# Saved tensors in another DRAM layout without row copies, and a forward softmax in two halves of heads, in a recurrent-memory transformer's forward and backward pass

## The chip, the cores and the metric

The kernel runs on one core of a Trainium2 chip. The core has a matrix engine (TensorE; in the profile PE for its matmuls, PEld for its weight loads), VectorE (DVE), ScalarE (ACT), GpSimd (POOL) and SyncE (SP), which here issues most of the DMAs (its queue is SPq in the rows). Sixteen DMA engines carry the transfers of the core. The metric is the device time of one execution in microseconds. Before: 2802.92 us, the median of three runs (2802.28 to 2803.98).

## The reference

The kernel computes a layer's output and all ten gradients (x, mem0, Wq, Wk, Wv, Wo, w1, b1, w2, b2) for a given grad_out. Cut to what matters:

```python
def _A_ref(x, mem0, Wq, Wk, Wv, Wo, seg_len):      # S 2048, Dm 512, 32 heads of 128, M 8, seg 32
    mask = (idx[:, None] < M) | (idx[:, None] >= idx[None, :])
    mem = mem0
    for s in range(S // seg_len):                  # 64 segments, one after the other
        h = concatenate([mem, x[:, s*32:(s+1)*32]], axis=1)      # 40 rows
        q, k, v = (einsum('btd,dhe->bhte', h, W) for W in (Wq, Wk, Wv))
        p = softmax(where(mask, q @ k^T * scale, -1e9))
        o = einsum('bhte,hed->btd', p @ v, Wo)
        mem = o[:, :M]                             # the memory of the next segment
        outs.append(o[:, M:])

def _B_ref(x, w1, b1, w2, b2):                     # F 1792
    return square(relu(x @ w1 + b1)) @ w2 + b2

xn = layernorm(x)
out = x + _A_ref(xn, ...) + _B_ref(xn, ...)        # and the gradients of all that by jax.vjp
```

## The kernel before

The work is done in five stages. First layer norm and the MLP, forward and the part of backward that needs no attention. Then the forward scan: 64 steps, one for each segment, each of which needs the memory that the step before gave. Four steps make a block (SPB = 4; 16 blocks, TC = 16). Then the attention weights are turned for backward. Then the backward scan over the 64 steps in the other direction. Last, the gradients of the four attention weights as large matmuls, which read what the scans saved in DRAM.

In a step 32 rows (RA; 8 of memory and the last 24 tokens) of 32 heads are worked on as 128 partitions by 1024 columns: the heads form four quarters (JQ = 4), quarter j on partitions 32 j to 32 j + 31, and 8 heads of 128 columns (NI = 8) lie side by side in a quarter. The first 8 tokens of each of a block's four segments ("L" rows, names that end in L) are computed once for a block, beside the chain of steps.

A forward step (`chain`, L1136) projects q, k and v (`proj`), copies them out of PSUM (`evict`, L526, one VectorE or ScalarE copy for 512 columns), transposes q and k on TensorE (`to_T`, L546), multiplies them into one PSUM bank of scores (`ps_sc`) on top of the mask, does softmax (`weights` L1003, `sums` L1012, `normalize` L1017), transposes the weights on VectorE, forms O = P V (`diag`, which scales by one over the sum), transposes O (`sq_T`), multiplies by Wo (`wo_part`) and turns the new memory into the next step's input (`ps_mem`). Into the gaps the stage puts matmuls of the MLP's weight gradients (`dw_unit`), whose inputs come as tiles `anT` and `sx`.

Each step saves to DRAM, by SyncE's queue: S_V, S_K, S_Q, S_P, S_ON (its O). Two DRAM-to-DRAM copies a step gather the memory rows of K and V (S_KM, S_VM) for the block's L rows. More row copies gather rows for the last stage (S_HNA, S_HNL, S_GOA, S_GOL) and the output's L rows (S_OL, S_BL).

A backward step loads those tensors (`load`: bP, VR by a transposing DMA, bqN, bkN), computes the gradients of q, k and v (dN, three of them, stored as S_GN), the parts of the L rows (eL, stored in S_GNL, read back as dLN) and the gradient of the layer's input.

The order of the three scheduled stages does not come from the code's order. Operations are recorded with their reads and writes and a cost for each engine that could do them; a planner (`_Plan`) lays them out in time with these costs, a rank along the longest path, a table of corrections for each operation (BIAS) and three numbers (PAR), and then emits them in the order it found. Each engine's queue is executed in that order. All DMAs that the steps name go through one helper (L477):

```python
def dma(self, out_f, in_f, R, W, prio=1, lat=3.2, cost=T_DMA, eng="SP"):
    q = {"SP": nc.sync, "POOL": nc.gpsimd, "ACT": nc.scalar}[eng]
    self.plan.add({eng: cost}, lambda e: q.dma_start(out_f(), in_f()), R, W, prio, lat)
```

so almost every DMA has line L479 in the profile, and copies out of PSUM have L433 (VectorE) or L435 (ScalarE).

Of the kernel before, what the change touches and what calls it, by code (L numbers as in the profile page):

```python
# [10 lines left out]
PAR = ((0.3, 0.3, 0.0), (0.61, 7.94, 4.04), (0.09, 2.05, 17.32))  # L11
BIAS_0 = None
BIAS_1 = {
    "l_proj": (
        47.2, 6.5, -41.1, 1.2, 0.8, -33.9, -14.2, 11.4, 20.3, -5.1, -5.3, -14.4, 17.4, 1.5, 7, 20.1, 4.7,
        25.3, -22.2, 55.6, -37, 19.3, -97.5, -1.4, 23, -6.1, -29.3, 48.8, 4.1, 4.5, 52.1, -159.3,
    ),
    "blk_in": (
        11.4, -35.6,
    ),  # L20
# [4 lines left out]
    ),  # L25
    "chain": (
# [4 lines left out]
    ),  # L31
    "blk_out": (
        16.8, -102.8, -36.2, -171.6, -10.2, -72.7, -50.6, -74.7, -96.5, 48.6,
    ),
    "l_attn": (
# [16 lines left out]
    ),  # L52
    "l_pre": (
        46.2, 1.1, -8.1, -100.3, 71, -115.1, -66.8, -4.6, 0.3, -83.5, 0.5, -9.3, -80.7, -12.7, -35.4, -15.9,
        26.3, 9.2, -131.2, 6, 10.9, -47, -9.6, -40.9, 6.9, -128.5, -6.9, -9.4, -61.5, 28.5, -31.2, -38.8,
        -146.2,
    ),
    "load": (
# [33 lines left out]

class _PE(dict):
    shape = None
    n = 8


def pe(cost, shape, n=8):
# [10 lines left out]
class _Plan:  # L109
# [56 lines left out]
    def run(self):  # L166
# [52 lines left out]
        while elig:  # L219
# [48 lines left out]
            if o.shape:  # L268
                shape = o.shape
# [1473 lines left out]
```

## Time and profile before

| what | value |
| --- | --- |
| time, median of three runs | 2802.92 us |
| the profiled execution: span from first to last instruction | 2798.3 us |
| TensorE busy | 2664.6 us (95%), clock 0.995 |
| VectorE / ScalarE / GpSimd busy | 1327.3 / 985.8 / 824.8 us |
| bytes moved by DMA | 530.91 MB, mean 190 GB/s |
| forward scan | about 228 to 1202 us |
| backward scan | about 1235 to 2225 us |
| weight gradients | about 2238 us to the end |

A row of the profile names line, engine, operation, tile written and tiles read, then a count and times. A window row (one for each stretch A:B) lists its length, then busy time and count of instructions of PE, PEld, DVE, ACT and POOL, the granted TensorE clock, the mean busy share of the sixteen DMA engines and GB/s. The bytes of a packet are put down where the packet starts. Issues of DMAs by SyncE are told in a timeline as start and duration of the issue, not of the transfer.

### The profile page before, as it was taken

What the parts mean: (1) busy time and instruction counts of PE and PEld (TensorE: products, weight loads), DVE (VectorE), ACT (ScalarE), POOL (GpSimd) and SP (SyncE); (2) the same over time, 40 slices, a digit from 0 to 9 for tenths busy, and PEclk for the clock granted to TensorE, in tenths of its full rate; (3) what the DMA queues carried; (4) which work ended last, traced back from release to release, by engine and by line L of the source; (5) the groups of instructions that cost most, each with busy time, mean ns of one, the idle gap of its engine ahead of it and who ended that gap; (6) DMA issues with size and microseconds to landing.
All of it is one profiled execution on the core that took longest, in us unless ns stands there. A gap on an engine that the chain in (4) does not pass through costs nothing.

```text
span 2798.3 us, 125071 instructions
## 1 busy us (share of the span) xinstructions
PE 2664.6 (95%) x54888; PEld 1538.5 (55%) x55072; DVE 1327.3 (47%) x3327; ACT 985.8 (35%) x2012; POOL 824.8 (29%) x2431
## 2 busy tenths in 40 slices
PE   8998999999999999999999999999999899999999
PEld 6664555555555555575555555555555444444444
DVE  5544455555455555565455455555455402232322
ACT  4333444444444444364444444444444300000000
POOL 1111111111111111145555555555555301112210
PEclk9999999999999999999999999999999999999999
DMA  6657656555557566647777676777766698788861
GB/s 211 202 172 205 180 160 175 164 166 163 156 169 186 169 185 175 177 118 178 187 181 187 179 189 179 189 192 190 188 182 177 201 344 273 232 255 270 257 185 42
DMA packets 499792, 530.91 MB, mean 190 GB/s; under 512 B 223845, under 2 KB 325398, under 8 KB 497070
## 3 DMA queue, kind: packets, MB, share of 16 engines
q1 hardware_dynamic: 480254, 463.06, 59.9%
q0 software_dynamic: 15056, 53.56, 5.6%
q8 instruction: 430, 7.05, 1.1%
q10 hardware_dynamic: 3936, 6.29, 0.7%
q14 instruction: 116, 0.95, 0.1%
HBM read 249.77 MB, written 237.52 MB: 174 GB/s over the span
## 4 chain that ended last, share of the span: by engine, by line
PE 45%; DVE 4%; issue 3%; DMA 3%; ACT 1%; POOL 1%; SPq 0%; DVEq 0%; ACTq 0%; POOLq 0%
PE ps_gw L1690 14%; PE ps_dRA L1370 8%; PE ps_gw L1694 5%; PE ps_gO L538 3%; PE ps_dRL L1370 3%; PE ps_d L624 2%; DMA dLN<-S_GNL 2%; PE ps_d L573 1%; PE ps_d L599 1%; PE ps_gOT L429 1%; PE ps_d L588 1%; PE ps_gm L1524 1%; PE ps_gL L538 1%; PE ps_dL L1481 1%; PE ps_dP L1468 1%
## 5 line engine op out<-in xcount | busy, mean ns | idle before, releaser
L1370 PE MATMUL ps_dRA<-WA,dT 128*32 128x512 bf16 x6144 | 377.0, 381 | 5.3 <-issue 2.5
L1690 PE MATMUL ps_gw<-WA,WB 128*128 128x512 bf16 x1505 | 330.6, 379 | 1.6
L1690 PEld LDWEIGHTS <-WB 128*128 128x128 bf16 x1896 | 185.4, 98 | 225.0 <-issue 1.7
L538 PEld LDWEIGHTS <-PA 128*32 128x32 bf16 x8192 | 195.4, 96 | 192.3 <-DVE PA L1190 22.3
L435 ACT CAST dN<-ps_d 128x512 bf16<-128x512 f32 x372 | 207.4, 590 | 184.7 <-PE ps_d L599 112.3
L1370 PEld LDWEIGHTS <-dT 128*32 128x32 bf16 x6144 | 151.8, 96 | 154.2 <-DVE dT L517 17.3
L433 DVE CAST gwo<-ps_gw 128x512 bf16<-128x512 f32 x64 | 40.0, 685 | 399.9 <-PE ps_gw L1690 268.5
L435 ACT CAST gwo<-ps_gw 128x512 bf16<-128x512 f32 x64 | 33.1, 598 | 510.2 <-PE ps_gw L1690 357.3
L517 DVE STREAM_TRANSPOSE dT<-dN 128x256 f32<-128x256 f32 x384 | 165.4, 437 | 72.1 <-ACT dN L435 66.5
L1020 POOL TENSOR_TENSOR P<-P,rsA 128x320 bf16<-128x320 bf16 x64 | 46.2, 722 | 458.8 <-DVE rsA L1015 244.1
L624 PEld LDWEIGHTS <-PB 32*32 32x32 bf16 x8192 | 119.8, 92 | 76.4 <-DVE PB L1168 23.9
L1701 POOL DMA_DIRECT2D out_dram<-gwo x96 | 71.6, 753 | 293.9 <-ACT gwo L435 265.1
L538 PE MATMUL ps_q<-WA,PA 128*32 128x512 bf16 x2048 | 145.2, 382 | 5.5 <-DVE PA L1190 3.7
L1039 PE MATMUL ps_RA<-WB,OT 128*32 128x256 bf16 x4096 | 129.0, 277 | 17.7 <-DVE OT L517 13.6
L538 PE MATMUL ps_k<-WA,PA 128*32 128x512 bf16 x2048 | 144.9, 381 | 0.3 <-DVE PA L1190 0.3
L435 ACT CAST kN<-ps_k 128x512 bf16<-128x512 f32 x125 | 73.4, 587 | 194.1 <-PE ps_k L538 172.2
L538 PE MATMUL ps_v<-WA,PA 128*32 128x512 bf16 x2048 | 140.7, 379 | 0.0
L1039 PEld LDWEIGHTS <-OT 128*32 128x32 bf16 x4096 | 103.9, 98 | 46.2 <-DVE OT L517 32.0
L538 PE MATMUL ps_gO<-WB,PA 128*32 128x512 bf16 x2048 | 126.4, 380 | 1.0 <-DVE PA L1528 1.0
L611 POOL COPY BDL<-bPLL 32x64 bf16<-32x64 bf16 x256 | 60.4, 236 | 218.4 <-PE ps_d L573 210.4
L433 DVE CAST qN<-ps_q 128x512 bf16<-128x512 f32 x62 | 42.9, 692 | 171.5 <-PE ps_q L538 169.5
L1254 PE MATMUL ps_dw<-sx,anT 128*128 128x512 bf16 x339 | 108.2, 384 | 6.6 <-DMA sx<-S_XN 2.8
(315 smaller groups left out, 5300.8 us busy)
## 6 DMA issues: line engine op xcount, KB each, us to landing
S_GN<-dN SPq DMA_DIRECT2D x192, 256.0 KB
WA<-S_GN SPq DMA_DIRECT2D x150, 256.0 KB
S_Q<-qN SPq DMA_DIRECT2D x64, 256.0 KB
S_K<-kN SPq DMA_DIRECT2D x64, 256.0 KB
S_V<-vN SPq DMA_DIRECT2D x64, 256.0 KB
S_ON<-oN SPq DMA_DIRECT2D x64, 256.0 KB
bqN<-S_Q SPq DMA_DIRECT2D x64, 256.0 KB
bkN<-S_K SPq DMA_DIRECT2D x64, 256.0 KB
```

The source lines that it names most:

```text
L433: nc.vector.tensor_copy(out, in_)
L435: nc.scalar.copy(out, in_)
L517: self.plan.add({"DVE": 0.445}, lambda e, half=half: nc.vector.transpose(words(dst, half).rearrange("p (i c r) -> p i c r", i=4, c=2), src ...
L538: nc.tensor.matmul(bk()[32 * j:32 * (j + 1), :], lhsT=win(dc), rhs=Wt(dc, c0), start=(dc == 0), stop=(dc == DC - 1), tile_position=(0, 32 ...
L611: f(q_(dst, j)[:, :, j, 0:c], q_(src_f(), j))
L624: nc.tensor.matmul(bk()[32 * j:32 * j + m, k * P:(k + 1) * P], lhsT=lf(j, i), rhs=rf(j, i), start=(k == 0 and x == 0), stop=(x == n - 1), ...
L1039: nc.tensor.matmul(bk()[32 * c:32 * (c + 1), :], lhsT=sg.rows(OTt, i, j), rhs=Wo[:, JQ * i + j, dh * DH:(dh + 1) * DH], start=(i == 0 and ...
L1254: nc.tensor.matmul(bks[x]()[:], lhsT=anT[x][:, c, :], rhs=sx[z][:], start=(c == 0), stop=(c == TC - 1))
L1370: nc.tensor.matmul(bk()[32 * j:32 * (j + 1), :], lhsT=sg.rows(XT, i, j), rhs=wtf(t, i, j), start=(first and i == 0), stop=(last and i == N ...
L1690: nc.tensor.matmul(bks[n](), lhsT=HNc[:, rc, dc * P:(dc + 1) * P], rhs=gns[y][:, hf * 512:(hf + 1) * 512], start=(y == 0), stop=(y == NRC ...
L1694: nc.tensor.matmul(bks[n](), lhsT=gns[y][:, k * P:(k + 1) * P], rhs=GOc[:, rc, :], start=(y == 0), stop=(y == NRC - 1))
L1701: nc.gpsimd.dma_start(outWs[t][dc * P:(dc + 1) * P, 4 * hf:4 * hf + 4, j, :], wt[:].rearrange("p (i e) -> p i e", i=4))
```

## The change

It has four parts. The order tables (PAR and BIAS) are replaced, and the planner now knows that some TensorE operations can be done in one of two tilings ("wf": one full 128 x 128 operation, or four of 32 columns), and picks the one that does not change the tiling in use.

The row copies go: the DRAM tensors that held gathered rows are no longer there. Instead the saved tensors have a layout from which both readers take rows with strided patterns, and only the memory rows of the layer's input are transposed and saved apart (S_HM, S_GM). The last stage loads its inputs HN and GO from S_XN, grad_out and these.

The forward softmax is done in two halves of heads, with a bank of scores each; q, k, their transposes and O leave PSUM in two pieces, each of which the planner gives to VectorE or ScalarE; two buffers of P (P40s) take turns.

The loads of sx, the MLP weight gradients' second input, come two blocks at a time from the GpSimd queue, and pairs of narrow matmuls on the L rows become one of twice the width.

```diff
-PAR = ((0.3, 0.3, 0.0), (0.61, 7.94, 4.04), (0.09, 2.05, 17.32))
+PAR = ((0.3, 0.3, 0.0), (0.0, 0.02, 42.99), (0.09, 14.67, 24.36))
...
-    S_K = dt_([NSEG, P, HW], BF16, "S_K")
-    S_V = dt_([NSEG, P, HW], BF16, "S_V")
+    S_K = dt_([TC, RA, JQ, SPB, HW], BF16, "S_K")
+    S_V = dt_([TC, RA, JQ, SPB, HW], BF16, "S_V")
...
-    S_VL = dt_([TC, P, HW], BF16, "S_VL")
-    S_KM = dt_([TC, P, HW], BF16, "S_KM")
-    S_VM = dt_([TC, P, HW], BF16, "S_VM")
+    S_VL = dt_([TC, M, JQ * SPB, HW], BF16, "S_VL")
...
-    S_ON = dt_([TC, P, SPB, HW], BF16, "S_ON")
-    S_ONL = dt_([NLC, P, BPC, HW], BF16, "S_ONL")
-    S_GN = dt_([3, TC, P, SPB, HW], BF16, "S_GN")
-    S_GNL = dt_([3, NLC, P, BPC, HW], BF16, "S_GNL")
+    S_ON = dt_([TC, JQ, SPB, RA, HW], BF16, "S_ON")
+    S_ONL = dt_([NLC, JQ, BPC, RL, HW], BF16, "S_ONL")
+    S_GN = dt_([3, TC, JQ, SPB, RA, HW], BF16, "S_GN")
+    S_GNL = dt_([3, TC, SPB, JQ, M, HW], BF16, "S_GNL")
+    S_HM = dt_([TC, DC, RL, P], BF16, "S_HM")
+    S_GM = dt_([TC, DC, RL, P], BF16, "S_GM")
...
+    def step_rows(t, s):
+        return t[s // SPB][:, :, s % SPB].rearrange("r j f -> j r f")
+
+    def mem_rows(t, b):
+        return t[b][0:M].rearrange("k j v f -> (j v) k f")
...
+        def evict2(self, out_f, bk, in_f, key, prio, cost, n=2):
+            self.plan.parts[key] = [(key, x) for x in range(n)]
+            for x in range(n):
+                c = slice(512 // n * x, 512 // n * (x + 1))
+                self.plan.add(cost, lambda e, c=c: ev({"DVE": "v", "ACT": "s"}[e], out_f(c), in_f(c)), [bk], [(key, x)], prio)
...
+            for h in range(2):
+                x, bk = slice(4 * h, 4 * h + 4), bks[h]
+                A({"DVE": 0.325}, lambda e, x=x, bk=bk: V.tensor_reduce(mx[:, x], bk()[:], axis=AX.X, op=ALU.max), [bk], [("mxA", h)], 0)
...
+                A({"ACT": 0.365}, lambda e, x=x: nc.scalar.activation(Et[:, x], st[:, x], ACT.Exp, scale=scale), [("stA", h)], [(pk, h)], 0)
...
-                for i in range(NI):
-                    for c in range(2):
-                        for j in range(JQ):
-                            nc.tensor.matmul(q_(ps, j)[:, i, 32 * c:32 * c + 32], lhsT=qLT[p][:, i, j, :],
-                                             rhs=KT[p][:, :, i * JQ + j, M * c:M * c + M],
...
+                    for j in range(JQ):
+                        nc.tensor.matmul(q_(ps, j)[:, i, :].rearrange("p (c v k) -> p v c k", c=2, k=M), lhsT=qLT[p][:, i, j, :],
...
-            sg.dma(lambda: S_V[s], lambda: flat(vN), [("vN", 0), ("vN", 1)], [("S_V", s)])
-            sg.dma(lambda: S_K[s], lambda: flat(kN), [("kN", 0), ("kN", 1)], [("S_K", s)])
+            sg.dma(lambda: step_rows(S_V, s), lambda: flat(vN), [("vN", 0), ("vN", 1)], [("S_V", s)])
+            sg.dma(lambda: step_rows(S_K, s), lambda: flat(kN), [("kN", 0), ("kN", 1)], [("S_K", s)])
...
-            sg.dma(lambda: part_of(S_ON, s, SPB), lambda: flat(oN), [("oN", 0), ("oN", 1)], [])
-            mrow = lambda t: t.rearrange("(j r) f -> j r f", j=JQ)
-            for nm, D_, S_ in (("S_V", S_VM, S_V), ("S_K", S_KM, S_K)):
-                sg.dma(lambda D_=D_: mrow(D_[b])[:, M * v:M * (v + 1), :], lambda S_=S_: mrow(S_[s])[:, 0:M, :],
-                       [(nm, s)], [(nm + "M", b, v)])
+            sg.dma(lambda: S_ON[b][:, v], lambda: flat(oN), [("oN", 0), ("oN", 1)], [])
...
-                sg.dma(lambda z=z: sx[z][:], lambda c=c: src[c * P:(c + 1) * P, :], [], [("sx", z)], lat=3.0)
+                z = c // 2 % 3
+                if c % 2 == 0:
+                    sg.dma(lambda z=z: sx[z][:], lambda c=c: src[c * P:(c + 2) * P, :].rearrange("(c p) d -> p c d", p=P), [], [("sx", z)], lat=3.2, cost=0.62, eng="POOL")
...
-            sg.dma(lambda: flat(kN), lambda: S_K[s], [], ["kN"], 0, lat=4.0)
+            sg.dma(lambda: flat(kN), lambda: step_rows(S_K, s), [], ["kN"], 0, lat=4.0)
...
-                sg.dma(lambda: part_of(S_GN[t], s, SPB), lambda: flat(dN[t]), both("dN%d" % t), [])
+                sg.dma(lambda: S_GN[t, b][:, v], lambda: flat(dN[t]), both("dN%d" % t), [])
```

What this does to the queues is seen in three places. A row of an order names the line, the operation, the tile written and the tile read (numbers behind a name tell buffers apart), and the pattern that is written. On SyncE, one step in the middle of the backward scan, before:

```order
L479 DMA S_GN<-dN_31376 128x1024
L479 DMA bkN<-S_K 128x1024
L479 DMA bPLL_31357<-S_PLL 128x512
L479 DMA S_R<-R_A 128x512
L479 DMA bqN<-S_Q 128x1024
L479 DMA S_GNL<-eL_31397 4x32x256
L479 DMA S_GN<-dN_31378 128x1024
L479 DMA S_GNL<-eL_31398 4x32x256
L1377 DMA_TRANSPOSE VR<-S_V 128x8x128
L479 DMA bP_31372<-S_P 128x320
L479 DMA S_GN<-dN_31377 128x1024
```

and the same place now (L503 is the changed kernel's line for a DMA, L1433 for a transposing one):

```order
L1433 DMA_TRANSPOSE VR<-S_V 128x8x128
L503 DMA S_GN<-dN_33949 4x32x1024
L503 DMA bkN<-S_K 128x1x1024
L503 DMA dLN<-S_GNL 128x1x1024
L503 DMA S_GN<-dN_33948 4x32x1024
L503 DMA bqN<-S_Q 128x1024
L503 DMA S_R<-R_A 128x512
L503 DMA S_GNL<-eL_33969 4x32x256
L503 DMA S_GN<-dN_33950 4x32x1024
L503 DMA S_GNL<-eL_33970 4x32x256
L1433 DMA_TRANSPOSE VR<-S_V 128x8x128
```

The stores of dN stand among the same loads as before, in nearly the same order; their written pattern is 4x32x1024 where it was 128x1024.

On SyncE, one step and a half of the forward scan, before:

```order
L479 DMA S_Q<-qN 128x1024
L479 DMA S_K<-kN 128x1024
L1244 DMA_TRANSPOSE anT_2676<-S_AT 128x8x128
L479 DMA S_KM<-S_K 4x8192
L479 DMA S_V<-vN 128x1024
L479 DMA S_P<-P_2661 128x320
L479 DMA S_ON<-oN 128x1024
L479 DMA sx_2681<-in_grad_out_dram 128x512
L479 DMA S_OL<-obL 32x256 x2
L479 DMA S_VM<-S_V 4x8192
```

and now:

```order
L503 DMA S_K<-kN 4x32x1024
L503 DMA S_Q<-qN 128x1024
L503 DMA obL<-S_B 32x1x256 x2
L503 DMA S_V<-vN 4x32x1024
L503 DMA S_P<-P_2656 128x320
L503 DMA S_VL<-vLN_2644 16x8x1024
L503 DMA S_ON<-oN 4x32x1024
L503 DMA S_QL<-lN_2647 128x1024
L503 DMA S_K<-kN 4x32x1024
```

The loads of sx and the copies into S_KM and S_VM are gone from this queue, and the stores of K, V and O have 4 outermost.

On VectorE, the middle of a forward step (scores to O), before:

```order
L433 CAST qN<-ps_q 128x512
L433 COPY qT<-ps_qT 128x512
L433 COPY KT_2646<-ps_kT 128x16x32 x2
L1007 TENSOR_REDUCE mxA<-ps_sc 128x8
L1008 TENSOR_TENSOR stA<-ps_sc,mxA 128x320
L1166 COPY PLp_2639<-P_2661 128x8x8
L1168 STREAM_TRANSPOSE PB<-P_2661 128x256
L1169 STREAM_TRANSPOSE PB<-PLp_2639 128x256
L1014 TENSOR_REDUCE smA<-P_2661 128x8
L1015 RECIPROCAL rsA<-smA 128x8
L994 TENSOR_REDUCE mxL<-ps_scL 128x8
L634 TENSOR_TENSOR oN<-ps_o,rsA 128x512
```

and now:

```order
L436 COPY qT<-ps_qT 128x256 x2
L1061 TENSOR_REDUCE mxA<-ps_sc 128x4
L1062 TENSOR_TENSOR stA<-ps_sc,mxA 128x160
L1061 TENSOR_REDUCE mxA<-ps_sc 128x4
L1062 TENSOR_TENSOR stA<-ps_sc,mxA 128x160
L1047 TENSOR_REDUCE mxL<-ps_scL 128x8
L1069 TENSOR_REDUCE smA<-P_2656 128x8
L1223 STREAM_TRANSPOSE PB<-P_2656 128x128
L1224 COPY PLp_2633<-P_2656 128x4x8
L1070 RECIPROCAL rsA<-smA 128x8
L1226 STREAM_TRANSPOSE PB<-PLp_2633 128x128
L1224 COPY PLp_2633<-P_2656 128x4x8
```

Each step of softmax stands there twice with half the columns, and a part of the q, k copies and of the scaling of O has moved to ScalarE or is in pieces of 256 columns.

More of the change, by code (lines that the diff above doesn't have):

```diff
@@ L94 @@
     shape = None
-    n = 8
+    n = {None: 8}
 def pe(cost, shape, n=8):
@@ L100, in pe @@
     x.shape = shape
-    x.n = n
+    x.n = {k: n * (4 if k == "w" and len(shape) > 1 else 1) for k in shape}
     return x
@@ L139, in add @@
         o.users = []
+        R, W = ([y for k in x for y in (k, *self.parts.get(k, ()))] for x in (R, W))
         R, W = ([k.key if isinstance(k, _Bank) and k.key else k for k in x] for x in (R, W))
@@ L225, in run @@
                 best = None
-                turn = o.shape not in (None, shape)
+                turn = bool(o.shape) and shape not in o.shape
                 g = _HOP + (0.0 if o.prio == 0 else self.grace)
@@ L285, in run @@
                     elig.append(u)
-            seq.append((o, e))
+            seq.append((o, form if form and len(o.shape) > 1 else e))
         assert len(seq) == len(ops)
@@ L592, in mixed, with mm0 @@
                 bk = bks[half]
+                if inter:
+                    def mm0(e, half=half, bk=bk):
+                        for k in range(4):
+                            for x, (lf, rf) in enumerate(pre):
+                                nc.tensor.matmul(bk()[:, k * P:(k + 1) * P], lhsT=lf(4 * half + k), rhs=rf(4 * half + k),
+                                                 start=(k == 0 and x == 0), stop=False, skip_group_check=True)
+                    self.plan.add(pe(0.22 * len(pre), "f", 4 * len(pre)), mm0, rkeys[0](half), [bk], prio, lift=lift)
                 def mm(e, half=half, bk=bk):
@@ new lines @@
+        for j in range(JQ):
+            nc.gpsimd.memset(mk[32 * j:32 * j + M, :], 0.0)
+        mkl = p0.tile([P, 2, SPB, M], BF16, name="mkl")
+        nc.gpsimd.memset(mkl[:], 0.0)
+        for j in range(JQ):
+            for c in range(2):
+                nc.gpsimd.affine_select(
+                    q_(mkl, j)[:, c], q_(mkl, j)[:, c], pattern=[[-M, SPB], [-1 if c == 0 else 0, M]],
+                    compare_op=ALU.is_ge, fill=NEG, base=0, channel_multiplier=1,
+                )
+                nc.gpsimd.affine_select(
+                    q_(mkl, j)[:, c], q_(mkl, j)[:, c], pattern=[[M, SPB], [0, M]],
+                    compare_op=ALU.is_ge, fill=NEG, base=M - 1, channel_multiplier=-1,
+                )
@@ L699 @@
+        for i in range(NI):
+            nc.vector.tensor_copy(maskA[:, i, M:KA], mk[:])
         RB = 2 * P
```

401 lines of the change are left out of this document (214 added, 187 removed), and 53 rows, old and new, of tables (BIAS_1, BIAS_2).

## The prediction

> **What bounds the kernel now.** I read the page's first two parts, then the step lengths, then a table of stages, then short stretches around single transfers. The page first:
>
> ```profile
> span 2798.3 us, 125071 instructions
> PE 2664.6 (95%) x54888; PEld 1538.5 (55%) x55072; DVE 1327.3 (47%) x3327; ACT 985.8 (35%) x2012; POOL 824.8 (29%) x2431
> PEclk9999999999999999999999999999999999999999
> DMA  6657656555557566647777676777766698788861
> ```
>
> TensorE is busy for 95% of the span at nearly full clock (tenths of full speed, never under 9), but the DMA row stands at 5 to 8 tenths almost everywhere: the second resource is not far behind. That row is a mean over sixteen engines. The profiled execution's span is 2798.3 us; the median of the shown runs is 2802.92, so 4.6 us lie outside the span. The sums below are differences and are added to the median.
>
> The two scans of 64 steps fill most of the span. The rows of the first projection of each step give their pace (nanoseconds min/median/max, then first and last start in us):
>
> ```profile
> L538 PE MATMUL ps_q<-WA,PA x2048: 376/379/634, 228.5 to 1192.4; 128*32 128x512 bf16 x187
> L538 PE MATMUL ps_gO<-WB,PA x2048: 376/379/391, 1235.5 to 2211.5; 128*32 128x512 bf16 x187
> ```
>
> Forward: 963.9 us over 63 intervals, 15.30 us a step. Backward: 976.0 over 63, 15.49 us. The table of stretches says what is busy inside forward, backward and weight gradients:
>
> ```profile
> core 0: us, PE busy (x) PEld busy (x) DVE busy (x) ACT busy (x) POOL busy (x), PEclk, DMA share, GB/s
> 235.00:1205.00 970.00, 907.98 (x23393) 542.31 (x23503) 513.94 (x1255) 427.56 (x885) 139.59 (x258) 0.99 0.61 172
> 1250.00:2200.00 950.00, 912.36 (x25816) 544.35 (x25816) 493.35 (x1228) 396.86 (x789) 525.88 (x1869) 1.00 0.72 183
> 2250.00:2780.00 530.00, 527.42 (x2408) 240.22 (x2455) 145.35 (x238) 31.98 (x62) 93.26 (x136) 1.00 0.76 237
> ```
>
> In the forward scan TensorE idles 970 - 908 = 62 us in all, in the backward scan 38, in the last stage under 3. TensorE bounds all three, so a shorter chain between its works can win at most those idle times. The mean DMA engine is busy 0.61 x 15.30 = 9.3 us of a forward step and 0.72 x 15.49 = 11.2 us of a backward step.
>
> **Part one: the DRAM shapes.** Removing the row copies turns the layout of the saved tensors round. These transfers, 256 KB each, are written before as 128 rows of 1024, and after as 4 x 32 rows on the DRAM side (the load of bkN reads such a pattern):
>
> ```profile
> S_GN<-dN SPq DMA_DIRECT2D x192, 256.0 KB
> S_K<-kN SPq DMA_DIRECT2D x64, 256.0 KB
> S_V<-vN SPq DMA_DIRECT2D x64, 256.0 KB
> S_ON<-oN SPq DMA_DIRECT2D x64, 256.0 KB
> bkN<-S_K SPq DMA_DIRECT2D x64, 256.0 KB
> S_GNL<-eL SPq DMA_DIRECT2D x128, 64.0 KB
> S_GNL<-dLN SPq DMA_DIRECT2D x64, 64.0 KB
> ```
>
> The last two have a pattern with 4 outermost already (4 x 32 x 256 and 4 x 8 x 1024). So before's trace shows both kinds alone. First what SyncE issued, then the stretches in which those transfers ran:
>
> ```profile
> 1566.69 1.28 SPq L479 DMA_DIRECT2D S_GNL<-dLN  x2
> 1568.06 0.41 SPq L479 DMA_DIRECT2D S_GN<-dN  x1
> 1709.85 0.52 SPq L479 DMA_DIRECT2D S_GNL<-eL  x1
> ```
>
> ```profile
> 1568.00:1568.90 0.90, 0.90 (x16) 0.45 (x16) 0.87 (x2) 0.00 (x0) 0.90 (x1) 1.00 0.26 80
> 1569.00:1569.60 0.60, 0.60 (x16) 0.13 (x12) 0.60 (x2) 0.04 (x1) 0.54 (x2) 1.00 1.00 372
> 1711.00:1711.93 0.93, 0.93 (x20) 0.36 (x12) 0.83 (x3) 0.00 (x0) 0.29 (x2) 1.00 0.32 86
> ```
>
> In the first and third stretch a store with 4 outermost keeps 0.26 and 0.32 of the sixteen engines busy, about four, at 80 and 86 GB/s. In the second the 128-row store S_GN<-dN has all of them (share 1.00) at 372 GB/s. It does not matter that the third stretch reads 128 partitions on the SBUF side.
>
> Are they always the same four? Two copies with 4 rows each stand one behind the other here (64 KB each, of V's and K's memory rows):
>
> ```profile
> 645.77 0.68 SPq L479 DMA_DIRECT2D S_VM<-S_V  x1
> 646.49 0.55 SPq L479 DMA_DIRECT2D S_KM<-S_K  x1
> ```
>
> ```profile
> 647.90:648.35 0.45, 0.45 (x16) 0.21 (x8) 0.00 (x0) 0.00 (x0) 0.00 (x0) 1.00 0.06 9
> 648.60:649.10 0.50, 0.50 (x16) 0.27 (x12) 0.00 (x0) 0.50 (x2) 0.00 (x0) 1.00 0.45 180
> ```
>
> The second is issued by 647.04, but between 647.90 and 648.35 almost nothing starts (9 GB/s; a packet's bytes count where it starts), with twelve engines free; at 648.60 it goes. So it queued behind the first on the same engines. I take the four as the same for every such transfer.
>
> The Trainium skill, page "DMA: Bandwidth & Descriptors", section "Why a DMA increments its semaphore by 16 and not by 1", states the same: the count of engines is the largest number up to 16 that divides the slowest dimension of both patterns, and the lowest-numbered engines get it. This trace agrees (0.26 and 0.32 of sixteen against 1.00), and the rule speaks against this change.
>
> The price: 256 KB at 372 GB/s is 0.70 us on each of sixteen engines; on four it is 2.82 us, 2.11 more on each of those four than before.
>
> **Backward.** Per step the mean engine has 11.2 us. The four already carry more than the mean: two eL stores, 128 KB at 80 GB/s, 1.6 us, 1.2 above what they would have if spread; one dLN store a step on average (64 KB), 0.8 us, 0.6 above. That is 13.0. Three S_GN stores and one bkN load add 4 x 2.11 = 8.4: 21.4 us a step on engines that have 15.49. They become the bound: 64 x (21.4 - 15.49) = +380 us. Nothing covers it: SyncE issues in order and has few transfers outstanding, so a load of the next step queues behind these stores. The price of one such store is taken at the pace of the 372 GB/s stretch. Bounds: if the mean 11.2 holds waiting between packets that vanishes when the other twelve are idle, I take off a fifth (2.2 us): 19.2, +237 us. If each step's chain also waits for its own loads, a tenth on top of 21.4: 23.5, +515 us.
>
> **Forward.** Mean 9.3; S_VM and S_KM (128 KB, 1.6 us) add 1.2 on the four: 10.5. They go (-1.6): 8.9. S_K, S_V and S_ON add 3 x 2.11 = 6.3; S_ONL, a quarter of one a step, 0.5: 15.7 us, against a pace of 15.30. So the scan ends about 64 x 0.4 = 26 us later, and cannot use what part two saves. Lower end: a fifth off the mean again (1.9) gives 13.8, no bound by DMA, and part two's gain stays (-31).
>
> **Part two: halves and pieces.** The chain of a forward step is shortened by overlapping: the reduce, subtract, exponential and transposes of the first four heads precede those of the others; q, k, qT, kT and O leave PSUM in two pieces, on two engines. The rows that are cut:
>
> ```profile
> L1007 DVE TENSOR_REDUCE mxA<-ps_sc 128x8 f32<-128x320 f32 x64 | 31.5, 492 | 51.5 <-PE ps_sc L1161 51.5
> L1008 DVE TENSOR_TENSOR stA<-ps_sc,mxA 128x320 f32<-128x320 f32 x64 | 31.5, 492 | 2.2
> L433 DVE CAST qN<-ps_q 128x512 bf16<-128x512 f32 x62 | 42.9, 692 | 171.5 <-PE ps_q L538 169.5
> L433 DVE COPY R_A<-ps_dRA 128x256 f32<-128x256 f32 x64 | 27.2, 424 | 171.8 <-ACT R_A L435 163.0 <-DMA S_GN<-dN 8.7
> ```
>
> From 692 ns for 512 columns and 424 for 256, a cut costs 2 x 424 - 692 = 156 ns. Five cut operations of softmax on VectorE add 0.8 us a step, some ten pieces of q, k, qT, kT and O at most 1.6 over VectorE and ScalarE. VectorE is busy 514/64 = 8.0 us of 15.3, ScalarE 6.7: the added work lies beside TensorE's. Were that cover gone, it would be 64 x 2.4 = 154 us; nothing says so. The gain is bounded by the 62 us of idle TensorE; with its filler work (weight gradients of the MLP) already in most gaps I take half, 31 us. In my forecast the four DMA engines swallow it.
>
> **Part three, the small edits.** 64 matmuls of 32 columns a block become 32 of 64, in two places:
>
> ```profile
> L1404 PE MATMUL ps_dPL<-VTL,LT 128*32 128x32 bf16 x512 | 10.9, 180 | 0.8 <-issue 0.7
> L1108 PE MATMUL ps_scL<-KT,qLT 128*32 128x32 bf16 x1024 | 10.7, 181 | 0.0
> L1701 POOL DMA_DIRECT2D out_dram<-gwo x96 | 71.6, 753 | 293.9 <-ACT gwo L435 265.1
> ```
>
> Half the count with wider matmuls: at most -5 us forward and -11 backward (the other half of ps_dPL has a row like the first); I take -5 for each where TensorE binds, nothing where DMA does. The 224 loads of sx become 112 issues on the GpSimd queue. GpSimd is busy 140 of 970 us forward; at 0.75 us an issue (the nearest row, the stores of gwo) 84 us more are covered. What waits behind such an issue there is the normalization of P and the addition to the output, which only stores follow: 0. The turn of weights, the MLP stage and the last stage keep their work; the last stage's rows of HN now come in many small pieces ahead of TensorE's start: +5 us, between 0 and 15.
>
> **The sum:** 2803 + 380 + 26 + 5 = 3214 us.
>
> **The rivals.**
> A, faster: the count of outer rows does not decide for a 256 KB store with 128 partitions and 2 KB rows, as it did for 512 B rows; it spreads over sixteen. Then part two's -31 and part three's -10 stand, +3 for the tail: 2803 - 38 = 2765. For it: no transfer of before has exactly this shape. Against it: the third stretch, 128 partitions and 4 outermost, 0.32 of sixteen. It decides if the four stay below 15.3 us a step. Chance 0.10.
> B, bound by four engines but lighter: the lower ends, +237 backward, forward -31 kept: 2803 + 237 - 31 + 5 = 3014; from there to 3120. For it: packets run quicker when twelve engines are idle. Against: the 372 GB/s stretch was itself taken at full share, and the four still write at their own pace. Chance 0.17.
> C, waits on top: +515 backward, and a tenth of 15.7 more forward (+126 instead of +26): 2803 + 515 + 126 + 5 = 3449. For it: SyncE's order puts loads behind stores, and late loads stop TensorE too. Chance 0.12; half of it lies above 3400.
>
> **How the numbers follow.** The forecast has 0.60, A 0.10, B 0.17, C 0.12, and 0.01 is left for a balance within 0.2% of before, which is about what a measurement of this kernel tells from no change. Faster 0.10, same 0.01, slower 0.89. The range from 3000 to 3400 holds the forecast's case, B and the nearer half of C; A and the far half of C are out.
>
> **What would show it.** Right: step intervals of about 21 us backward and 15.7 forward; the mean DMA share falling to about 0.5 in the backward scan while SyncE's DMAs queue; TensorE idle for a quarter there, waiting for loads (VR, bkN, dLN) and for buffers that stores hold (dN); the last stage as long as before. Wrong: a stretch with a lone S_GN<-dN at a share near 1.00 refutes the step on the four engines; a scan under 15.3 us a step means A; a backward step near 19 means that the mean was taken too high; VectorE or ScalarE as the releaser of most idle TensorE time forward would mean that the pieces cost what I hid.

## The result, and the profile after

The changed kernel takes 3336.78 us (3325.31 to 3337.99, 4 runs), the kernel before 2803.45 in the same session: a ratio of 1.189 (95% interval 1.187 to 1.191), 533 us more. The forecast was 3214, 411 more; the range of 3000 to 3400 holds the result. Of all executions behind the numbers below, one (of the kernel with S_VM and S_KM on eight engines) took 8901 us and does not enter its ratio. From the page of the changed kernel:

```profile
span 3336.1 us, 129735 instructions
PE 2794.2 (84%) x56752; PEld 1608.5 (48%) x56752; DVE 1435.0 (43%) x4050; ACT 1010.7 (30%) x2317; POOL 929.0 (28%) x2572
PEclk9999999999998999988899999898989888999999
DMA  6667666677676664367776766766676658988981
DMA packets 469532, 517.55 MB, mean 155 GB/s; under 512 B 221793, under 2 KB 288626, under 8 KB 467426
```

Fewer bytes move (517.55 MB against 530.91), more slowly, TensorE's share falls from 95 to 84%, and its clock is no longer full all through. The step lengths say where the time is (nanoseconds min/median/max, first and last start):

```profile
L568 PE MATMUL ps_q<-WA,PA x2048: 379/379/634, 232.1 to 1396.4; 128*32 128x512 bf16 x187
L568 PE MATMUL ps_gO<-WB,PA x2048: 376/379/634, 1437.3 to 2728.6; 128*32 128x512 bf16 x187
```

Forward: 1164.3 us over 63 intervals, 18.48 us a step where it was 15.30. Backward: 1291.3, 20.50 where it was 15.49. So 200 us of the loss lie in the forward scan and 315 in the backward scan. From the last backward step to the end it is 607.5 us against 586.8, 21 more; the first stage and the turn together cost 1.

The stretches of both scans, columns as before (length, busy time and count of PE, PEld, DVE, ACT and POOL, granted clock, DMA share, GB/s):

```profile
250.00:1380.00 1130.00, 931.47 (x24324) 558.36 (x24320) 561.12 (x1854) 446.51 (x1172) 216.89 (x365) 0.94 0.65 132
1450.00:2700.00 1250.00, 970.23 (x25512) 572.97 (x25508) 530.52 (x1271) 377.25 (x740) 542.46 (x1878) 0.91 0.70 137
```

In a backward step TensorE idles (1250 - 970.2) / 1250 of 20.50, 4.6 us, where it idled 0.6. It is also busy for longer, 15.9 us instead of 14.9, with nearly the same work: the granted clock is 0.91.

One backward stall shows how the lost time comes about. On VectorE, in order (start, length, work, and in brackets the idle time before and what ended it):

```profile
1623.09 0.28 DVE L436 CAST maskL<-ps_gN 128x128 bf16<-128x128 f32 x1
1636.58 0.77 DVE L541 STREAM_TRANSPOSE LT<-dLN 128x256 f32<-128x256 f32 x2 [13.21 <-DMA dLN<-S_GNL]
1637.28 0.72 DVE L436 COPY gOT<-ps_gOT 128x512 bf16<-128x512 bf16 x2
```

On SyncE at the same time, what was issued ahead of that load of dLN and the load itself:

```profile
1617.55 3.21 SPq L503 DMA_DIRECT2D S_GNL<-dLN  x3
1620.87 0.39 SPq L503 DMA_DIRECT2D bP<-S_P  x1
1621.36 0.55 SPq L503 DMA_DIRECT2D S_GN<-dN  x1
1622.01 1.32 SPq L1433 DMA_TRANSPOSE VR<-S_V  x1
1623.42 1.12 SPq L503 DMA_DIRECT2D S_GN<-dN  x1
1624.64 1.97 SPq L503 DMA_DIRECT2D bkN<-S_K  x1
1626.71 2.26 SPq L503 DMA_DIRECT2D dLN<-S_GNL  x1
```

And the engines in the last ten microseconds of it:

```profile
1628.00:1630.00 2.00, 0.00 (x0) 0.00 (x0) 0.00 (x0) 0.00 (x0) 0.00 (x0) 0.94 0.60 150
1634.00:1636.00 2.00, 0.00 (x0) 0.00 (x0) 0.00 (x0) 0.00 (x0) 0.00 (x0) 0.50 0.26 96
```

Six transfers with 4 outermost stand ahead of the load (three dLN stores, two of dN, bkN). The load itself has 128 rows and is spread over all sixteen engines, so I read the end of the stall as its part on the four, which comes last: at 1634 to 1636 the share is 0.26, and all five engines stand still. VectorE stands at the transpose of dLN, which belongs to the L rows, and behind it in its queue is gOT, which the chain needs; TensorE waits for gOT. The tables of waits, over the whole run, have for dLN before, and for dLN, gOT and bqN now (waiting engine and tile, what it waited for, us in all, times, longest):

```profile
DVE LT L517 <- DMA dLN<-S_GNL: 49.1, 24, 6.5
```

```profile
DVE LT L541 <- DMA dLN<-S_GNL: 220.4, 28, 13.7
PE ps_dP L1523 <- DVE gOT L436: 120.4, 25, 11.1
PE ps_d L648 <- DMA bqN<-S_Q: 48.1, 26, 4.6
```

The other two rows are of TensorE; before, neither is among its largest.

### The profile page after: what moved, and what is told of

Same layout as the page of the kernel before. It is cut to its first block, busy times and chain, and to the rows that moved or that the text cites. A ratio compares the mean times of both kernels' runs of the same rounds, so it can differ in the third digit from the quotient of the medians.

```text
span 3336.1 us, 129735 instructions
## 1 busy us (share of the span) xinstructions
PE 2794.2 (84%) x56752; PEld 1608.5 (48%) x56752; DVE 1435.0 (43%) x4050; ACT 1010.7 (30%) x2317; POOL 929.0 (28%) x2572
## 2 busy tenths in 40 slices
DMA packets 469532, 517.55 MB, mean 155 GB/s; under 512 B 221793, under 2 KB 288626, under 8 KB 467426
## 4 chain that ended last, share of the span: by engine, by line
PE 34%; DMA 15%; issue 4%; DVE 3%; ACT 1%; SPq 0%; POOL 0%; ACTq 0%; DVEq 0%; POOLq 0%; another core or an unknown queue 0%
PE ps_gw L1752 12%; DMA dLN<-S_GNL 7%; PE ps_dRA L1426 7%; DMA bqN<-S_Q 6%; PE ps_gw L1756 4%; PE ps_dRL L1426 3%; PE ps_d L674 2%; PE ps_gO L568 1%; PE ps_d L648 1%; PE ps_dL L1536 1%; DMA WB<-S_HM 1%; PE ps_dP L1523 1%; DMA V<-S_K 1%; PE ps_d L611 0%; PE ps_gm L1579 0%
## 5 line engine op out<-in xcount | busy, mean ns | idle before, releaser
L1426 PE MATMUL ps_dRA<-WA,dT 128*32 128x512 bf16 x6144 | 402.0, 401 | 43.8 <-issue 25.4
L568 PEld LDWEIGHTS <-PA 128*32 128x32 bf16 x8192 | 217.5, 99 | 195.5 <-issue 43.0
L1426 PEld LDWEIGHTS <-dT 128*32 128x32 bf16 x6144 | 160.9, 101 | 214.7 <-issue 64.1
L1094 PE MATMUL ps_RA<-WB,OT 128*32 128x256 bf16 x4096 | 138.3, 279 | 38.2 <-DVE OT L541 32.2
L1311 PE MATMUL ps_dw<-sx,anT 128*32 128x512 bf16 x1768 | 132.4, 401 | 45.1 <-DMA sx<-in_grad_out_dram 21.1
L661 POOL COPY BDP<-bP 32x256 bf16<-32x256 bf16 x256 | 100.9, 394 | 196.1 <-PE ps_d L611 180.2
L541 DVE STREAM_TRANSPOSE LT<-dLN 128x256 f32<-128x256 f32 x96 | 40.2, 422 | 239.3 <-DMA dLN<-S_GNL 220.4
L568 PE MATMUL ps_q<-WA,PA 128*32 128x512 bf16 x2048 | 136.4, 384 | 3.5 <-ACT lN L438 3.5
L1523 PE MATMUL ps_dP<-bVT,gOT 128*32 128x40 bf16 x2048 | 36.3, 187 | 121.8 <-DVE gOT L436 120.4
L1426 PE MATMUL ps_dRL<-WA,LT 128*32 128x512 bf16 x1536 | 131.0, 456 | 0.0
```

The costliest lines, as they stand in the source:

```text
L541: self.plan.add({"DVE": 0.445}, lambda e, half=half: nc.vector.transpose(words(dst, half).rearrange("p (i c r) -> p i c r", i=4, c=2), src ...
L568: nc.tensor.matmul(bk()[32 * j:32 * (j + 1), :], lhsT=win(dc), rhs=Wt(dc, c0), start=(dc == 0), stop=(dc == DC - 1), tile_position=(0, 32 ...
L661: f(q_(dst, j)[:, :, j, 0:c], q_(src_f(), j))
L1094: nc.tensor.matmul(bk()[32 * c:32 * (c + 1), :], lhsT=sg.rows(OTt, i, j), rhs=Wo[:, JQ * i + j, dh * DH:(dh + 1) * DH], start=(i == 0 and ...
L1311: nc.tensor.matmul(bks[x]()[m:m + w, :], lhsT=anT[x][:, c, m:m + w], rhs=sx[z][:, c % 2, :], start=(c == 0), stop=(c == TC - 1), tile_posi ...
L1426: nc.tensor.matmul(bk()[32 * j:32 * (j + 1), :], lhsT=sg.rows(XT, i, j), rhs=wtf(t, i, j), start=(first and i == 0), stop=(last and i == N ...
```

## The experiments

Twelve kernels. The steps are first starts of ps_q and ps_gO, as above; the ratio is to the kernel before in the same session, with its 95% interval. The kernel before took 2799.31 to 2807.62 us in these sessions (medians), and a loss named below is the difference to its own session's.

| kernel | time, us | ratio | forward step | backward step |
| --- | --- | --- | --- | --- |
| before | 2803.45 | 1 | 15.30 | 15.49 |
| after | 3336.78 | 1.189 (1.187 to 1.191) | 18.48 | 20.50 |
| before, dN on four engines | 3018.58 | 1.075 (1.072 to 1.078) | 15.35 | 18.85 |
| before, dN on two engines | 3315.26 | 1.182 (1.179 to 1.185) | 15.32 | 23.34 |
| before, dN in four DMAs | 2913.56 | 1.038 (1.036 to 1.041) | 15.33 | 17.19 |
| before, O on four engines | 2866.51 | 1.022 (1.020 to 1.024) | 16.63 | 15.33 |
| the same, O issued by ScalarE | 2932.76 | 1.047 (1.044 to 1.050) | 17.66 | 15.40 |
| the same, O issued by GpSimd | 2845.30 | 1.016 (1.011 to 1.021) | 16.06 | 15.30 |
| before, S_VM and S_KM on eight engines | 2801.53 | 0.999 (0.9975 to 1.0004) | 15.27 | 15.47 |
| after, all split in four DMAs | 3057.86 | 1.089 (1.087 to 1.091) | 16.03 | 18.53 |
| after, backward split | 3203.94 | 1.141 (1.138 to 1.144) | 18.30 | 18.49 |
| after, forward split | 3189.81 | 1.135 (1.133 to 1.138) | 16.18 | 20.36 |
| after, all split, whole evictions | 3020.24 | 1.076 (1.073 to 1.079) | 15.65 | 18.42 |
| after, stores of 128 rows | 2928.52 | 1.043 (1.040 to 1.046) | 16.40 | 16.08 |

### Does the count of outer rows set the count of engines?

The kernel before, with unused rows in S_GN so that 32 (or 64) rows don't join the next ones; the later loads stay contiguous. The first kernel's edit is shown; the second has `[3, TC, 2, 65, SPB, HW]` and `0:64`:

```diff
-    S_GN = dt_([3, TC, P, SPB, HW], BF16, "S_GN")
+    S_GN = dt_([3, TC, 4, 33, SPB, HW], BF16, "S_GN")
...
-                sg.dma(lambda: part_of(S_GN[t], s, SPB), lambda: flat(dN[t]), both("dN%d" % t), [])
+                sg.dma(lambda: S_GN[t, b][:, 0:32, v], lambda: flat(dN[t]), both("dN%d" % t), [])
```

> The kernel before with one thing changed: S_GN has one unused row after each 32, so that the three stores of dN have 4x32x1024 as their written pattern instead of 128x1024; what is read later is still contiguous. Theory: the four engines have 11.2 + 1.8 + 3 x 2.11 = 19.3 us a backward step, 64 x 3.8 = 244 us more, 3047 us; the forward step stays at 15.3. Rival (the count of outer rows does not matter for a 256 KB store): 2803 within 0.3%.

> The kernel before with one unused row after each 64 in S_GN: dN's stores have 2x64x1024. Theory (the count of outer rows is the count of engines): 5.64 us a store on two engines; 13.0 + 3 x 4.94 = 27.8 us a backward step, 3590 us. Rival (rows that don't join, not their outer count, made the 4x32 pattern slow): as with 4x32, about 3020 us.

The first lost 211 us, with the backward step at 18.85 (19.3 expected) and the forward step as it was. The second lost 509, clearly more than the first, so it is the count and not that rows don't join. Stretches of one microsecond with the share of such a store alone, first of the kernel with two engines, then of the changed kernel:

```profile
1546.00:1547.00 1.00, 1.00 (x42) 0.90 (x41) 0.36 (x2) 0.91 (x2) 0.00 (x0) 1.00 0.13 51
1547.00:1548.00 1.00, 1.00 (x63) 0.79 (x62) 0.46 (x2) 0.82 (x3) 0.55 (x3) 1.00 0.13 51
```

```profile
1556.00:1557.00 1.00, 1.00 (x24) 0.41 (x20) 1.00 (x3) 0.00 (x0) 0.96 (x3) 1.00 0.26 102
1557.00:1558.00 1.00, 1.00 (x20) 0.37 (x12) 0.90 (x2) 0.00 (x0) 0.71 (x1) 1.00 0.26 102
```

A share of 0.13 is two of sixteen, 51 GB/s; 0.26 is four, 102 GB/s: some 25 GB/s an engine in both. How full these engines are over a whole scan can be bounded by counting, from every packet's start and duration, the packets under way at once. With dN on two engines, fewer than two were under way for 0.3% of the backward scan (before: 14%), so nothing speaks against two engines that never rest. In the changed kernel fewer than four were under way for 4% of it (before: 18%); for that time at least, the four cannot all have been busy. But 3590 us was expected on two engines and 3315 came.

### What the changed kernel loses by it

Each of these transfers as four DMAs of 32 rows, one behind the other on SyncE, in the place of the one:

```diff
+        def dma4(self, dram_f, sb_f, R, W, prio=1, lat=3.2, cost=T_DMA, load=False):
+            def go(e):
+                d, t = dram_f(), sb_f()
+                for j in range(JQ):
+                    o, i = (q_(t, j), d[j]) if load else (d[j], q_(t, j))
+                    nc.sync.dma_start(o, i)
...
-            sg.dma(lambda: step_rows(S_V, s), lambda: flat(vN), [("vN", 0), ("vN", 1)], [("S_V", s)])
+            sg.dma4(lambda: step_rows(S_V, s), lambda: flat(vN), [("vN", 0), ("vN", 1)], [("S_V", s)])
```

> Each store of K, V, O and dN and each load of bkN is issued as four DMAs of 32 rows, one for each quarter, so that every one has 32 rows outermost instead of 4; layouts, planner and order stay. Theory (four of sixteen engines carry these transfers and bound both scans): they spread again, forward step at or below 15.3 us, backward at or below 15.5, in all 2765 to 2810 us. Rival one (the loss comes from the rest of the change: pieces, order, sx on the GpSimd queue): above 3200. Rival two (four times the issues on SyncE, 3.2 us a step more forward and 4.2 backward, take the place of the bound): 2850 to 3000.

> As the last one, but only dN's stores and the load of bkN are split. Theory: the backward step falls from 20.5 to about 15.5 us and the forward step stays at 18.5, about 3015 us. Rival (the forward scan's late stores also delay the backward scan, or the other way round): the parts do not add up.

> Only the stores of K, V and O (and the L rows' O) are split. Theory: the forward step falls from 18.5 to at most 15.3 us and backward stays at 20.5, about 3130 us. Rival (the forward loss, eight times what was forecast, comes from sx on the GpSimd queue and the pieces): still above 3280, with the forward step above 17.5 us.

All split: 3057.86, so 279 us are back, but not the 530 of the theory, and more is lost than rival two said. The two parts miss their times in the same direction (3203.94 for 3015, 3189.81 for 3130); they bring 133 and 147, together 280: they add up. Forward the step falls to 16.03; backward only to 18.53. There SyncE has become nearly full: its issues take 83% of the backward scan (57% before), and its pauses of more than 0.15 us add up to 7% (37% before). In this stretch no issue waits for anything but the one before:

```profile
1865.31 1.93 SPq L510 DMA_DIRECT2D S_GN<-dN  x4
1867.33 0.53 SPq L503 DMA_DIRECT2D S_GNL<-eL  x1
1867.97 0.60 SPq L503 DMA_DIRECT2D V<-S_K  x1
1868.66 0.54 SPq L503 DMA_DIRECT2D bP<-S_P  x1
1869.29 1.28 SPq L1441 DMA_TRANSPOSE VR<-S_V  x1
1870.67 2.32 SPq L510 DMA_DIRECT2D S_GN<-dN  x4
1873.08 1.77 SPq L510 DMA_DIRECT2D bkN<-S_K  x4
```

To see what the issues cost alone, the kernel before with the same helper for dN's stores, which were on sixteen engines already:

> The kernel before with each store of dN issued as four DMAs of 32 rows: nine more issues on SyncE a backward step, nothing else. SyncE has about 24 issues in two steps of its old queue, with pauses. Theory A (issues cost 0.45 us each on SyncE and it fills up): 4 us more of 15.5, some of it in pauses, 1 to 2 us a step or 2870 to 2930 us. Rival (issues are free as long as SyncE has pauses, and the split kernel's remaining loss has another cause): 2803 to 2815 us.

It lost 108 us, 1.70 a step for nine more issues of 0.42 us each (the median), and SyncE's issues take 83% of its backward scan too. Theory A holds.

The other way to spread them needs no more issues: S_GN, S_ON and S_K laid out as before, and the inputs of the last stage taken with a stride of 4 over the partitions, to match the order of rows. V's store and the load of K's memory rows are split.

```diff
-    S_GN = dt_([3, TC, JQ, SPB, RA, HW], BF16, "S_GN")
+    S_GN = dt_([3, TC, P, SPB, HW], BF16, "S_GN")
...
-            ops.append((t[RA * v + M:RA * (v + 1), c0:c1, :], ...
+            ops.append((t[SPB * M + v:P:SPB, c0:c1, :], ...
```

> The changed kernel with S_GN, S_ON and S_K laid out as before (128 rows a store, one DMA each); the last stage's inputs HN and GO are loaded with a stride of 4 over the partitions instead, so no row copies come back; only V's store is split in four. Theory A (what is left in the kernel with all stores split, 18.5 us a backward step, is SyncE's issue time, since it issues without a pause there): backward at most 15.6 us, forward 15.5 to 16.0, in all 2790 to 2850 us. Rival (the rest of the change costs the backward scan 3 us a step by itself, by its order or its other layouts): backward stays at 18 or more, above 2980 us.

Backward 16.08 us: of the 5.0 us lost a step, 4.4 came from these transfers. Forward 16.40; the sum, 2928.52, missed the expected 2790 to 2850, since neither scan came quite down. Forward it is even above the kernel with everything split (16.03). One difference is the store of O's L rows, which still has 4 outermost here; no run says whether that is the reason.

### Is it the full engines, or the wait for a late store?

Forward the bound had been put at 15.7 us, and the step was 18.48. So the smallest case: the kernel before with O's store alone on four engines (S_ON with 33 rows a quarter).

> The kernel before, with one unused row after each 32 in S_ON, so that O's store alone has 4x32x1024. The prediction's bound: the four engines have 10.5 + 2.1 = 12.6 us of a 15.30 us forward step, so nothing changes, 2803 us. Rival (a store on four engines delays the step by what waits behind it, long before the four are full): 0.3 us or more a step, 2825 us or above.

61 us lost, 1.33 us a step, with four engines that by the prediction's sum had work for 12.6 of 15.3 us. The bound was wrong here, and a late store costs before the engines are full: fewer than four packets were under way for 16% of this forward scan, so the four had time left. In the order of the program (not a measurement) each DMA of SyncE names what it waits for:

```
L479 DMA S_KL<-lN_2654 128x1024 [waits DMAHW1_49,Activation_49]
L479 DMA obA<-S_B 32x4x256 [waits DMAHW2_49]
L479 DMA S_P<-P_2661 128x320 [waits DMAHW3_49,Pool_49]
```

The DMAs of SyncE and ScalarE take eight completion semaphores (DMAHW0 to 7) in turn, and one is used again only when its last DMA has ended. The trace of before bears out the turn: its DMAs of SyncE name eight semaphores, and 2572 of the 2583 steps from one to the next go to the next of the eight. In the run above SyncE waited 27.6 us for S_ON's stores. So two runs with another issuer:

```diff
-            sg.dma(lambda: S_ON[b][:, 0:32, v], lambda: flat(oN), [("oN", 0), ("oN", 1)], [])
+            A({"SP": T_DMA}, lambda e: nc.scalar.dma_start(S_ON[b][:, 0:32, v], flat(oN)), [("oN", 0), ("oN", 1)], [], 1, 3.2)
```

> As the run with S_ON alone on 4x32x1024 (+61 us), but O's store is issued on ScalarE's queue, at the place where it stood on SyncE's. Theory (SyncE issues in order with few transfers outstanding, and the late store of O holds up the loads behind it): SyncE's waits on S_ON and S_K shrink and the loss falls below 25 us. Rival (the other transfers wait on the four DMA engines themselves, whoever issues the store): the loss stays at 50 to 70 us.

> S_ON alone on 4x32x1024 once more, O's store now issued by GpSimd, at the place where it stood on SyncE's queue. In the order of the program each DMA of SyncE or ScalarE takes the next of eight completion semaphores and waits until that one's last DMA has ended; GpSimd's DMAs have others. Theory (that wait of SyncE for the late store is the loss: it stood still for 204 us on it when ScalarE issued it): without it the loss falls below 25 us, forward step at most 15.6 us. Rival (the store's packets hold up other transfers on the same engines, whoever waits): 50 us or more lost, forward step at 16.1 or more.

ScalarE's queue doubled the loss (17.66 us a step), which neither theory said. There SyncE's wait for the store has grown from 27.6 us. In the tables of waits from 250 to 1230 us it stands so, with a wait of TensorE that comes of it:

```profile
SPq L479 <- DMA S_ON<-oN: 204.3, 42, 8.0
PE ps_oL L624 <- DMA VM<-S_VM: 32.8, 6, 8.5
```

A stall shows it. In the timelines of ScalarE's and SyncE's queues, O's store and SyncE's last issue before and first issue after:

```profile
725.07 0.53 ACTq L1201 DMA_DIRECT2D S_ON<-oN  x1
724.46 0.38 SPq L479 DMA_DIRECT2D S_K<-kN  x1
730.88 0.34 SPq L479 DMA_DIRECT2D VM<-S_VM  x1
```

```profile
727.00:728.00 1.00, 0.00 (x0) 0.00 (x0) 0.00 (x0) 0.00 (x0) 0.00 (x0) 0.71 0.25 51
728.00:729.00 1.00, 0.00 (x0) 0.00 (x0) 0.00 (x0) 0.00 (x0) 0.00 (x0) 0.50 0.24 80
729.00:730.00 1.00, 0.00 (x0) 0.00 (x0) 0.00 (x0) 0.00 (x0) 0.00 (x0) 0.50 0.23 90
```

A quarter of the DMA engines is busy for three microseconds, and nothing else. SyncE stands from 724.84 to 730.88: the load of VM waits for the semaphore that O's store was given, and takes it over. TensorE waits for that load, 8.5 us, the longest in the row above.

With GpSimd as the issuer (its own eight semaphores) no wait of SyncE names O's store, and the loss was 46 us by the medians, 0.76 a step in the profiled execution: not under 25 and not over 50. Against the 61 us with SyncE the gain is small for the noise: the intervals of the two ratios just touch, though each of the four times is below each of the other four. So the wait for the late store is, by these runs, part of the loss, and the larger part stays when that wait is gone. What TensorE waits for there in the forward scan:

```profile
PE ps_dw L1254 <- DMA sx<-S_XN: 15.9, 10, 4.7
PE ps_oL L624 <- DMA VM<-S_VM: 10.7, 7, 3.4
```

Before, these two were 2.8 and 2.0 us, and with O's store issued by SyncE 18.1 and 11.7. That fits the rival, loads whose part on the four engines comes late whoever waits, but it does not prove it: what GpSimd's own issues cost, and which engines its DMAs take, was not tried apart.

### The smaller terms

> The changed kernel with all stores split, whose forward step is 16.03 us, and in it the pieces undone: q, k, their transposes and the scaling of O leave PSUM in one instruction of 512 columns, on the engine and at the place that the planner chose for the first piece; softmax stays in halves. Theory (the pieces cost more than they bring): forward step at 15.3 to 15.7 us, 20 us or more gained. Rival (the pieces shorten the chain, and the rest of the forward loss is issue time on SyncE): forward step at 16.4 us or more, 20 us or more lost.

In the changed kernel with all stores split, each piece pair is one again over 512 columns (the planner's second piece does nothing; ScalarE scales O in four instructions of 128, as in the kernel before). The forward step fell from 16.03 to 15.65 us, 24 us over 64 steps, and the time from 3057.86 to 3020.24. TensorE's wait for the transposed O up to 1200 us, with the pieces and without:

```profile
PE ps_RA L1102 <- DVE OT L549: 29.1, 57, 1.3
PEld L1102 <- DVE OT L549: 64.7, 90, 1.4
```

```profile
PE ps_RA L1104 <- DVE OT L549: 16.9, 45, 1.3
PEld L1104 <- DVE OT L549: 42.8, 93, 1.4
```

In this order, which was planned for them, the pieces cost more than they bring, most visibly at O.

At last the transfers of before that had 4 outermost, the copies of memory rows, with the dimensions exchanged so that 8 stand outermost:

```diff
-                sg.dma(lambda D_=D_: mrow(D_[b])[:, M * v:M * (v + 1), :], lambda S_=S_: mrow(S_[s])[:, 0:M, :],
+                sg.dma(lambda D_=D_: mrow(D_[b])[:, M * v:M * (v + 1), :].rearrange("j r f -> r j f"), lambda S_=S_: mrow(S_[s])[:, 0:M, :].rearrange("j r f -> r j f"),
```

> The kernel before with the two copies of memory rows a forward step (S_VM, S_KM) written as 8 x 4 x 1024 instead of 4 rows of 8192: eight engines instead of four. Theory (every transfer on four engines costs the step about half of its extra time): 0.4 us less on the four for each, so 0.2 to 0.4 us a step, 10 to 25 us less, 2780 to 2795 us. Rival (forward is bound by TensorE, and transfers that small are hidden): 2803 within 0.2%.

A ratio of 0.999 with 1 inside the interval: at 64 KB they are hidden, the rival is right. No kernel tried here beats the one before by more than can be measured.

## Why the prediction was right, step by step

**The four engines**: right. The share of 0.13 with two outer rows and 0.26 with four is the count of engines, and 4.4 of the 5.0 us lost in a backward step come back when the stores have 128 rows again. The rule of the Trainium skill, page "DMA: Bandwidth & Descriptors", section "Why a DMA increments its semaphore by 16 and not by 1", was quoted for four; the case of two agrees (51 GB/s on a share of 0.13). Rival A (a 256 KB store with 2 KB rows spreads anyway) is refuted by the first padded kernel.

**The price of one transfer**: 2.82 us on four engines by 372 GB/s over sixteen; the lone stretches give 102 GB/s, 2.57 us, a tenth less.

**The backward sum**: 21.4 us a step forecast, 20.50 measured, 321 us of the 380. Two errors in it went against each other. The base of 13.0 us, taken from a mean DMA share, was too high: with dN on two engines a step is 23.34 us, and three stores at 51 GB/s take 3 x 5.14 = 15.4 of them, which leaves at most 7.9 for all other work of these two, where the prediction had 10.9. That is rival B's doubt, and it was right about the base. One reason can be read from the packets: the share adds up their times, and more than sixteen are under way at once for 25% of the backward scan of before, so some engines' time is counted twice. On the other side rival C's waits are real: SyncE's queue and VectorE's queue pass a late load on to the chain, and TensorE's work itself grew by 1.0 us a step by the lower clock. By 7.9 + 3 x 2.57 = 15.6, an estimate from these figures, the kernel with dN on four engines would hardly be bound, and it took 18.85. Whether its four engines rested for the difference is open: the trace does not name a packet's engine, and fewer than four packets were under way for only 5% of that scan. So that 21.4 came so near to 20.50 was partly luck, and the sign named for a base taken too high (a backward step near 19) did not come, because the other error hid it.

**The forward sum**: the term that was mis-sized. It was 26 us, and 200 were measured. The same reading of a bound, 15.7 against 15.3, left out that a store on four engines delays the step before they are full: O alone cost 1.33 us a step where the sum gave none, and the three stores together at least 2.3 to 2.5 us (from 18.48 to 16.18 and 16.03, with the price of splitting still in it). The prediction named the mechanism, "a load of the next step queues behind these stores", for backward, and then priced forward without it.

**Part two**: hidden, the prediction said, with a gain of up to 31 us if DMA did not bind. The run without pieces shows a loss of about 0.4 us a step instead. The cover named (VectorE at 8.0 of 15.3 us) was there; the pieces lie on the chain all the same, and the chain has no cover at O. Whether the halves of softmax by themselves gain was not tried.

**Part three**: moving sx to the GpSimd queue was put at nothing, and that holds. In the changed kernel TensorE waits 45 us of the forward scan for loads, 40 of them for sx, but with all stores split it waits 6 us for all loads, with sx still on that queue. The wider matmuls were not tried apart.

**What is left**: with all stores split and the pieces undone, 0.35 us a forward step remain (15.65 against 15.30). More issues on SyncE, the new order and the halves are the candidates; no run separates them. Backward 0.6 us remain in the kernel with stores of 128 rows. The last stage was put at 5 us more, at most 15, and took 21; no run says why.

**The signs named ahead**: the backward step came near to what was said (20.5 for 21), the forward step did not (18.5 for 15.7). TensorE idles 22% of the backward scan ("a quarter"), waiting for dLN as named, through gOT, and for bqN, which was not. The mean DMA share did not fall to 0.5: it is 0.70, with fewer GB/s. It counts packets' time, and their time grew. The last sign, VectorE or ScalarE as the releaser of most of TensorE's idle time forward, came: 115 of 196 us. But before it was 36 of 48, so it tells little; the run without pieces tells more.

## What to carry to other kernels

Before a DRAM layout is changed, look at the outermost count of every transfer that follows from it, on both sides: a layout that saves copies can put the large transfers on a quarter of the DMA engines. Then don't price such a transfer by whether its engines fill up: in a queue that issues in order, with a few transfers outstanding, the slowest one can delay what stands behind it. Splitting it into several DMAs mends the engines and is paid in issue time; a layout with many rows outermost spares the extra issues (backward 16.08 us a step against 18.53 with the stores split; forward it brought no more than splitting, 16.40 against 16.03), and a stride on the other side, here over partitions, lets the later stage still read it.

## What the runs showed of the hardware

Short idle stretches cost more than their length. In the changed kernel TensorE waited in a forward step for a late sx, and its own rows show what the restart is like (start, length):

```profile
823.00 1.47 PE L1311 MATMUL ps_dw<-sx,anT 128*32 128x512 bf16 x24
829.79 1.04 PE L1311 MATMUL ps_dw<-sx,anT 128*32 128x512 bf16 x8 [5.30 <-DMA sx<-S_XN]
830.60 2.80 PE L568 MATMUL ps_k<-WA,PA 128*32 128x512 bf16 x24
```

```profile
827.00:828.00 1.00, 0.00 (x0) 0.00 (x0) 0.00 (x0) 0.00 (x0) 0.00 (x0) 0.82 0.25 84
832.00:833.00 1.00, 1.00 (x16) 0.42 (x12) 0.00 (x0) 0.36 (x1) 0.00 (x0) 0.50 1.18 101
834.00:835.00 1.00, 1.00 (x21) 0.41 (x13) 0.00 (x0) 0.00 (x0) 0.00 (x0) 0.77 0.66 51
```

The granted clock falls from 1.00 to 0.50 some three microseconds after TensorE stops at 824.5, and is back only 4.7 us after it starts again at 829.8: 24 matmuls take 2.80 us instead of 1.47. In the whole run the clock falls 68 times, and 67 of these half-speed stretches last a whole multiple of 3.41 us. The Trainium skill, page "TensorE: Matmul & The Clock Gate", section "Part 1: The HAM clock gate (the "warmup" mystery)", gives half the clock after at least one idle window of about 3.4 us and the full one after a busy window, and says that the windows run free of the kernel. This trace agrees in the half and in the length of the window. But the fall can come sooner than 3.4 us: in the stall with O's store on ScalarE's queue it came 2.2 us after TensorE's last matmul. The 1.0 us by which TensorE's busy time grew in a backward step goes with the mean clock of 0.91 there.

A transposing DMA also takes longer to issue when large stores keep few DMA engines busy. SyncE's rows for anT (nanoseconds min/median/max), before and after:

```profile
L1244 SPq DMA_TRANSPOSE anT<-S_AT x28: 1232/1297/2484, 242.4 to 718.9; - x28
```

```profile
L1298 SPq DMA_TRANSPOSE anT<-S_AT x28: 1370/3064/5792, 240.5 to 702.0; - x28
```

With all stores split the median is 1408 again, with stores of 128 rows 1392. The backward scan's VR has a median of 1268 ns before, 2682 with dN on four engines and 5395 with dN on two. So slow stores cost twice here: they land late, and SyncE is held longer at each transposing load behind them. What SyncE waits for in that time, the rows do not say.
